# Two steps' attention scores in one block, and the attention values in a feed-forward PSUM bank

## The chip, the cores and the metric

The kernel runs on one core of a Trainium2 chip. The metric is device time in microseconds (us) for one execution, median of three runs. The core has five engines that work side by side, each through a queue of its own in program order: TensorE (PE, matrix products; its weight loads are listed as PEld), VectorE (DVE), ScalarE (ACT), GpSimd (POOL), and SyncE (SP), which here only issues DMAs. Products land in PSUM, which has eight banks of 512 fp32 columns by 128 partitions; ACT and DVE read them from there.

## What is computed

Top-k attention over 8 batches x 8 heads x 576 positions x 64 features, then a feed-forward block over the 4608 tokens. Everything is fp32 at the kernel's edge.

```python
scores = scale * np.matmul(q, k.transpose(0, 1, 3, 2))            # 576 x 576 for each batch and head
kth = np.partition(scores, -32, axis=-1)[..., -32:-31]            # the 32nd largest of each row
scores = np.where(scores >= kth, scores, -1e9)
scores = scores - scores.max(-1, keepdims=True)
attn = np.exp(scores); attn = attn / (attn.sum(-1, keepdims=True) + 1e-9)
x = (attn @ v).transpose(0, 2, 1, 3).reshape(4608, 512)
h = x @ w_in                                                      # 512 -> 2048
out = (h - np.tanh(h)) @ w_out                                    # 2048 -> 512
```

## The kernel before

**Steps.** Attention is cut into 144 steps. A step is one pair of heads by 128 query rows: the pair's two heads are `t` = 0 and 1. 576 is 4 x 128 + 64, so the last 64 query rows of two head pairs make a "rem" step of their own. Steps come in groups of two (`nq` = 2, two row blocks of one head pair) whose values are computed together; a unit of feed-forward work is 256 tokens (128 for a few), and is ready when the values of its four head pairs are there. One batch is 18 steps.

**The loop.** The order of all instructions is written out by the Python loop `for n in range(-4, NS + LAG)`; no scheduler moves them inside it. In turn n the loop issues work of several steps:

- `mask(n - 1)`: POOL makes the threshold (`tb`, L334), ACT a relu against it (L347), POOL a subtraction (L350) and a check (`bad`, L354).
- `search(n)`: DVE finds the 32nd largest score of each row. It folds the near half of the keys, read from PSUM (`ps`), with the far half, read from the SBUF copy (`sc`): L297 to L305; then rounds of MAX8 and MATCH_REPLACE8 (L309 to L319). Between the rounds lie the reciprocal of step n - 2 (`invert`, L389 on DVE), its scaling on ACT (`divide`, L396), and its 32x32 transposition on DVE (`turn_z`, L427).
- `spread_keys(n - 2)`: SP sends the transposed weights to DRAM and back into the layout that the value products want (`there`, then `et` or `spare`).
- `deal(0.4)`: a share of the waiting feed-forward work.
- `scores(n + 1)`: PE makes the scores of the next step (L267), ACT copies them to SBUF (L275).
- `expo(n - 1)`: ACT's exponentials with their sums (L370); POOL adds the epsilon (`rd`, L380).
- three times `deal(0.2)`, and the loads and transpositions of q and k and the loads of v that are due.

**Values.** `values(m)` runs five turns after its group's last step (`LAG`): ten pairs of products on PE (L492) into PSUM, and a copy by ACT into the unit's input `xT` (L512). From turn `NEAR` = 45 on it stands directly ahead of `scores`; before that, at the start of the turn.

**Feed-forward.** Work is dealt in items of equal PE time. `ffn_h` is one item of 8 products (16 records in the trace, since an fp32 product shows as two); two items fill a bank, and then ACT makes tanh (L555) and a copy (L556) from it, and POOL subtracts them (L557). `ffn_o` adds up one 128-token block of the output over 8 items in one bank; ACT copies it (L574) and SP stores it. `rate()` sets how many items a turn gets, from the turns at which units become ready.

**PSUM.** Eight banks: four for the scores of one step (`ps[P, 2, 2, 512]`: two heads by two halves of 288 keys), two in turn for `zt` (transpositions early on, and the values `av`), two in turn for the feed-forward (`h_ps`).

**Shapes of products.** Feed-forward products use all 128 rows and 128 columns of PE's array. Score products have 64 rows (the head's features), and two run side by side, one in each half of the rows; value products have 64 columns, and two run side by side in the halves of the columns. The trace names them 128\*128, 64\*128 and 128\*64 (64\*64 for the scores of rem steps).

Of the kernel before, what the change touches and what calls it, by code (L numbers as in the profile page):

```python
# [10 lines left out]
FP32 = mybir.dt.float32  # L11
# [10 lines left out]

NEAR = 45


# [26 lines left out]
def kernel(  # L52
# [49 lines left out]
    sc_ps = pool("sc_ps", 1, space=PS)  # L102
    zt_ps = pool("zt_ps", 2, space=PS)
    h_ps = pool("h_ps", 2, space=PS)

# [34 lines left out]
    def convert(piece, slot):  # L140


        j, i = piece // CD, piece % CD
        if j < WJ:
            src, dst = moe_w_in[i * P : (i + 1) * P, j * NW : (j + 1) * NW], w_in[j][:, i, :]
        else:
            r0 = ((j - WJ) * FJ + i) * P
            src, dst = moe_w_out[r0 : r0 + P, :], w_out[j - WJ][:, i, :]
        raw, shifted, _ = slot
        nc.sync.dma_start(flat(raw), src.bitcast(U32))  # L150
        nc.sync.dma_start(
            flat(shifted).bitcast(U8)[:, 0 : 8 * NW - 4], src.bitcast(U8)[:, 3 : 8 * NW - 1]
        )
# [7 lines left out]
        e = h_ps.tile([P, NW], FP32, tag="h", name="e")[:] if j < WJ else f[:]  # L161
# [12 lines left out]
        yield  # L174
# [56 lines left out]
    def turn_rows(name, b, hp):  # L231
# [7 lines left out]
        for c0, c1, w in ((0, J, P), (J, J + 1, R)):  # L239
            zt = zt_ps.tile([P, 512], FP32, tag="zt", name="zt")  # L240
            for c in range(c0, c1):
# [14 lines left out]
    rest = consts.tile([P, 2, S4 + Q], FP32, name="rest")  # L256

    def scores(n):
        g = steps[n]
        ps = sc_ps.tile([P, 2, 2, 512], FP32, tag="sc", name="scps")  # L260
        for s in range(2):
            ks = slice(s * S2, (s + 1) * S2)
            for i in range(2 if g.rem else 1):
                qs = slice(JP, S) if g.rem else slice(g.qt * P, (g.qt + 1) * P)
                rows = half(i) if g.rem else slice(0, P)
                for t in range(2):
                    nc.tensor.matmul(  # L267
                        ps[rows, t, s, 0:S2],
                        qT[g.b, g.hp + i][half(t), qs],
                        kT[g.b, g.hp + i][half(t), ks],  # L270
                        start=True,
                        stop=True,
                    )
        sc = scpool.tile([P, 2, 2, S2], FP32, tag="sc", name="sc")
        nc.scalar.copy(sc[:], ps[:, :, :, 0:S2])  # L275
        st[n] = dict(sc=sc, ps=ps)

    def search(n, exact, between):
# [5 lines left out]
        x = st[n]  # L284
        sc, ps = x["sc"], x.pop("ps")
        m = x["m"] = mpool.tile([P, 2, TOP], FP32, tag="m", name="m")
# [6 lines left out]
        else:  # L293
            top = x["top"] = tpool.tile([P, 2, S4 + Q], FP32, tag="top", name="top")
            near, far = ps[:, :, 0, 0:S2], sc[:, :, 1, :]
            a, b = half_max, ps[:, :, 0, S2 : S2 + S4]
            nc.vector.tensor_tensor(b, near[:, :, S4:], far[:, :, S4:], ALU.max)  # L297
# [151 lines left out]
    def turn_pe(n):  # L449
# [10 lines left out]
        for k0 in range(0, KC, J):  # L460
            kn = min(J, KC - k0)
            zt = zt_ps.tile([P, 512], FP32, tag="zt", name="zt")
            for k in range(kn):
# [13 lines left out]

    def values(n):


        g = steps[n]
        nq, u = g.nq, g.unit
        et = tiles(ets.pop(n), nq)
        w = nq * P
        av = zt_ps.tile([P, 2, N], FP32, tag="zt", name="av")
        for i in range(2 if g.rem else 1):
# [3 lines left out]
            for c in range(J + 1):  # L490
                for t in range(2):
# [5 lines left out]
                        stop=(c == J),  # L497
                    )
        if g.pe:
            rx = rxs.pop(n)  # L500
# [32 lines left out]
    def ffn_h(u, item):  # L533
# [3 lines left out]
        for f in range(item * per, (item + 1) * per):  # L537
            j, fo = f // FJ, (f % FJ) * P
            s = f * w % 512
            if s == 0:  # L540
                cur[u] = h_ps.tile([P, 512], FP32, tag="h", name="hps")
            for c in range(CD):
# [7 lines left out]
        if item % 2:  # L550
# [3 lines left out]
            g = u.g[-1][:, item % 4 // 2, :]  # L554
            nc.scalar.activation(th[:], cur[u][:], AF.Tanh)  # L555
            nc.scalar.copy(g, cur[u][:])  # L556
            nc.gpsimd.tensor_tensor(g, g, th[:], ALU.subtract)  # L557

    def ffn_o(u, i, part):
        if part == 0:  # L560
            cur[u] = h_ps.tile([P, DM], FP32, tag="h", name="ops")
        for f in range(2 * part, 2 * part + 2):
            o = f * u.n + i * P
            nc.tensor.matmul(  # L564
                cur[u][:],
                u.g[o // 1024][:, o % 1024 // 512, o % 512 : o % 512 + P],
# [6 lines left out]
        ot = thpool.tile([P, DM], FP32, tag="th", name="ot")  # L573
        nc.scalar.copy(ot[:], cur[u][:])  # L574
        for rows, dst in u.blocks[i]:
# [51 lines left out]
    def run(exact):  # L627
# [10 lines left out]
        for i, (b, hp) in enumerate(pairs):  # L638
            n = next(n for n, g in enumerate(steps) if (g.b, g.hp) == (b, hp))
            for x, name in enumerate("kq"):  # L640
                m = max(n - 5 + x, turned.get(name, -4))
                if b == 0 and not exact:
# [106 lines left out]

        for n in range(-4, NS + LAG):  # L750
            pe = here(-2) and steps[n - 2].pe
            def due():
                for m in (n - LAG, n - LAG + 1, n - LAG + 2):
                    if 0 <= m < NS and steps[m].last and steps[m].lag == n - m:
                        values(m)

            if n < NEAR:
                due()
            share, usable = rate(), converted[0]
# [15 lines left out]
            if n >= NEAR:  # L775
                due()
            if here(1):
                scores(n + 1)
            if pe:
# [20 lines left out]
    nc.vector.reduce_max(any_bad[:], bad[:].rearrange("p t n i -> p (t n i)"), axis=mybir.AxisListType.X)  # L800
    cnt = zt_ps.tile([P, 512], FP32, tag="zt", name="cnt")
    nc.tensor.matmul(cnt[0:1, 0:1], any_bad[:], ones[:], start=True, stop=True)
# [35 lines left out]
```

## Time and profile before

| | |
|---|---|
| median of 3 runs | 1512.03 us (1511.23 to 1512.41) |
| the profiled execution's own time | 1509.65 us |
| its span, first to last instruction | 1507.5 us |
| mean granted TensorE clock | 0.982 |
| busy, share of the span | PE 95%, DVE 86%, ACT 67%, POOL 58% |
| largest groups | `ffn_o` products 517.5 us, `ffn_h` products 466.7 us, score products 189.0 us, value products with 256 columns from `et` 62.3 us and from `spare` 54.5 us |
| ACT copy of a step's scores | 1114 ns, 144 times |

The median stands 2.4 us above the profiled execution's own time, and that stands 2.15 us above its span. "Busy" counts a matmul from its start to its modelled end, so that PE at 100% can still hold gaps between the starts of its products; those are read from the rows in order of time. A wait is idle time of an engine together with what released it.

### The profile page before, as it was taken

The page shows a single profiled execution, that of the slowest core. Times are in us where ns is not written, and L with a number is a line of the kernel's source. Part 1 is how long each engine was busy: PE and PEld are TensorE (multiplying, and loading weights), DVE is VectorE, ACT ScalarE, POOL GpSimd, SP SyncE. Part 2 cuts the span into 40 slices and gives each one's busy share as a digit, 9 for nine tenths or more (in the row PEclk, how much of TensorE's full clock was granted, in tenths as well). Part 3 has the DMA queues.
Part 4 walks back from the last instruction along what each step waited for, and adds up shares of the span by engine and source line. Part 5 has one row for each costly group of instructions (what it writes and reads, how often), then busy time and mean ns, then how long its engine had stood idle before and what let it go on. Part 6 is the DMA issues. An engine that isn't in the chain of part 4 may idle for free.

```text
span 1507.5 us, 25020 instructions
## 1 busy us (share of the span) xinstructions
PE 1426.5 (95%) x7332; PEld 908.2 (60%) x7332; DVE 1295.2 (86%) x4886; ACT 1004.9 (67%) x1813; POOL 879.1 (58%) x1370
## 2 busy tenths in 40 slices
PE   4667898999999999999999999999999999999998
PEld 2454656465666565656565665657575675656673
DVE  7999899999998999999989999899988989886100
ACT  4766777777776777777676676768676676766220
POOL 3777667566565575657565575747474664646120
PEclk9888999999999999999999999999999999999999
DMA  9954123657854685567655865466554766443400
GB/s 277 373 170 167 25 43 92 171 156 153 205 147 140 164 166 156 134 176 171 162 136 146 175 147 165 138 166 159 156 145 117 174 144 177 111 140 105 109 7 17
DMA packets 248563, 221.68 MB, mean 147 GB/s; under 512 B 190816, under 2 KB 197984, under 8 KB 241248
## 3 DMA queue, kind: packets, MB, share of 16 engines
q1 hardware_dynamic: 246640, 219.75, 56.0%
q8 instruction: 61, 1.00, 0.3%
q14 instruction: 86, 0.70, 0.2%
q10 hardware_dynamic: 1776, 0.22, 0.1%
HBM read 136.17 MB, written 83.76 MB: 146 GB/s over the span
## 4 chain that ended last, share of the span: by engine, by line
PE 74%; DVE 15%; ACT 4%; POOL 2%; DMA 2%; issue 1%; SPq 0%; ACTq 0%; DVEq 0%; POOLq 0%
PE ops L564 28%; PE hps L543 28%; PE av L492 9%; PE scps L267 8%; DVE m L316 3%; DVE top L309 2%; DVE rest L319 2%; DVE zx L427 2%; DVE ab L303 1%; DMA w_in<-in_k_dram 1%; DVE f L170 1%; PE zt L464 1%; DVE f L159 1%; DVE top L319 1%; DVE ab L298 1%
## 5 line engine op out<-in xcount | busy, mean ns | idle before, releaser
L564 PE MATMUL ops<-w_out,g 128*128 128x512 f32 x1152 | 517.5, 600 | 2.4 <-POOL bad L354 1.5
L543 PE MATMUL hps<-xT,w_in 128*128 128x256 f32 (+1 forms) x2176 | 466.7, 372 | 1.0 <-ACT g L556 0.9
L350 POOL TENSOR_TENSOR z<-sc,z 128x576 f32<-128x576 f32 x288 | 404.5, 1426 | 86.2 <-ACT z L347 86.2
L543 PEld LDWEIGHTS hps<-xT,w_in 128*128 128x128 f32 x2176 | 392.0, 192 | 75.8 <-issue 21.6
L564 PEld LDWEIGHTS ops<-w_out,g 128*128 128x128 f32 x1152 | 213.3, 191 | 262.3 <-issue 250.3
L347 ACT ACTIVATE z<-sc,tb 128x576 f32<-128x576 f32 x288 | 207.6, 769 | 141.9 <-POOL tb L334 141.2
L557 POOL TENSOR_TENSOR g<-g,th 128x512 f32<-128x512 f32 x144 | 183.6, 1277 | 145.7 <-ACT g L556 140.9
L396 ACT ACTIVATE z<-z,rd 128x576 f32<-128x576 f32 x252 | 180.7, 764 | 97.0 <-DVE rd L389 96.9
L370 ACT ACTIVATE z<-z,nb 128x576 f32<-128x576 f32 x288 | 221.6, 774 | 2.5 <-POOL z L350 2.4
L380 POOL TENSOR_SCALAR rd<-den 128x2 f32<-128x2 f32 x144 | 32.7, 227 | 312.9 <-ACT z L370 307.1
L267 PE MATMUL scps<-kT,qT 64*128 64x288 f32 (+1 forms) x1280 | 189.0, 447 | 18.4 <-DVE qT L237 8.2
L427 DVE STREAM_TRANSPOSE zx<-z 128x1152 f32<-128x1152 f32 x126 | 172.0, 1365 | 35.2 <-ACT z L396 34.6
L309 DVE MAX8 top<-ab 128x8 f32<-128x144 f32 x864 | 194.6, 295 | 0.0
L275 ACT COPY sc<-scps 128x1152 f32<-128x1152 f32 x144 | 160.4, 1114 | 41.8 <-PE scps L267 41.4
L316 DVE MAX8 m<-rest 128x8 f32<-128x168 f32 x576 | 161.6, 322 | 0.0
L267 PEld LDWEIGHTS scps<-kT,qT 64*128 64x128 f32 (+1 forms) x1280 | 102.4, 184 | 94.5 <-issue 19.9
L316 DVE MAX8 m<-top 128x8 f32<-128x144 f32 (+1 forms) x576 | 151.7, 305 | 0.0
L555 ACT ACTIVATE th<-hps 128x512 f32<-128x512 f32 x144 | 84.2, 585 | 64.5 <-PE hps L543 62.1
L303 DVE TENSOR_TENSOR ab<-scps,sc 128x576 f32<-128x576 f32 x144 | 107.6, 748 | 0.0
L297 DVE TENSOR_TENSOR scps<-scps,sc 128x288 f32<-128x288 f32 x144 | 64.6, 449 | 46.1 <-ACT sc L275 45.7
L354 POOL TENSOR_SCALAR bad<-top,tb 128x3 uint8<-128x3 f32 x288 | 95.0, 341 | 0.0
L492 PE MATMUL av<-et,vb 128*64 128x256 f32 (+1 forms) x640 | 76.8, 372 | 18.2 <-ACT et L467 18.2
(78 smaller groups left out, 1536.8 us busy)
## 6 DMA issues: line engine op xcount, KB each, us to landing
there<-zx SPq DMA_DIRECT2D x56, 1152.0 KB, 4.2
spare<-there SPq DMA_DIRECT2D x112, 288.0 KB, 4.7
et<-there SPq DMA_DIRECT2D x112, 288.0 KB, 5.2
kin<-in_k_dram SPq DMA_DIRECT2D x116, 72.0 KB, 2.9
vb<-in_v_dram SPq DMA_DIRECT2D x64, 128.0 KB, 5.9
out_dram<-ot SPq DMA_DIRECT2D x32, 256.0 KB, 3.3
qin<-in_q_dram SPq DMA_DIRECT2D x113, 72.0 KB, 3.7
there<-zx SPq DMA_DIRECT2D x14, 576.0 KB, 5.2
```

Of the source, the lines that this page charges most:

```text
L267: nc.tensor.matmul(ps[rows, t, s, 0:S2], qT[g.b, g.hp + i][half(t), qs], kT[g.b, g.hp + i][half(t), ks], start=True, stop=True,)
L309: nc.vector.max(top[:, t, o : o + 8], low[:, t, i, :])
L316: nc.vector.max(m[:, t, m8], seen[i][t])
L347: nc.scalar.activation(zv[:, t, :], scf[:, t, :], AF.Relu, bias=tb[:, t : t + 1], scale=-BIG)
L350: nc.gpsimd.tensor_tensor(zv[:, t, :], scf[:, t, :], zv[:, t, :], ALU.subtract)
L370: nc.scalar.activation(x["zv"][:, t, :], x["zv"][:, t, :], AF.Exp, bias=x["nb"][:, t : t + 1], scale=scale, accum_out=den[:, t : t + 1],)
L396: nc.scalar.activation(x, x, AF.Copy, scale=rds[n][:, g.i, t : t + 1])
L427: nc.vector.transpose(tiles(zx, g.nq)[:, :, :, g.i, :].rearrange("p c k j -> p k c j"), z[:].rearrange("p (k c j) -> p k c j", c=NG, j=G),)
L492: nc.tensor.matmul(av[half(t), 0, cols], vb[g.b, hp][:, t, c, :] if c < J else vr[g.b, hp][:, t, :], es[:, :, (J + 1) * t + c if c < J els ...
L543: nc.tensor.matmul(cur[u][:, s : s + w], w_in[j][:, c, fo : fo + P], u.xT[:, c, 0:w], start=(c == 0), stop=(c == CD - 1),)
L557: nc.gpsimd.tensor_tensor(g, g, th[:], ALU.subtract)
L564: nc.tensor.matmul(cur[u][:], u.g[o // 1024][:, o % 1024 // 512, o % 512 : o % 512 + P], w_out[f // FJ][:, f % FJ, :], start=(f == 0), sto ...
```

## The change

From turn 18 on (`PAIRS`), the scores of two steps are made in one go in every even turn, and none in the odd ones. The four score banks now hold, for each of the two steps and heads, keys 0 to 319 (`WIDE`); the remaining 256 keys of both steps go into the two `zt` banks. ACT's one copy of 1152 columns for a step becomes three, of 640, 256 and 256. DVE's scratch in the score banks moves to columns 320 to 463.

Since the `zt` banks are taken, the values are put into whichever of the two feed-forward banks is not in use, `hbs[last_hb[0] ^ 1]`. Values that would be due in an odd turn wait for the next even one, where a rem step's may join others in the same bank. From turn 45 on they stand directly ahead of the scores of two steps. `zt` and feed-forward banks are now four fixed tiles that `zt_bank()` and `h_bank()` hand out in turn. q and k are loaded and transposed one turn earlier.

```diff
-    zt_ps = pool("zt_ps", 2, space=PS)
-    h_ps = pool("h_ps", 2, space=PS)
+    zt_ps = pool("zt_ps", 1, space=PS)
+    h_ps = pool("h_ps", 1, space=PS)
+    zts = [zt_ps.tile([P, 512], FP32, name=f"zt{i}")[:] for i in range(2)]
+    hbs = [h_ps.tile([P, 512], FP32, name=f"hb{i}")[:] for i in range(2)]
+    last_zt, last_hb = [0], [0]
+    def zt_bank():
+        last_zt[0] ^= 1
+        return zts[last_zt[0]]
+    def h_bank():
+        last_hb[0] ^= 1
+        return hbs[last_hb[0]]
...
+    def scores_of_two(n):
+        ps = sc_ps.tile([P, 2, 2, 512], FP32, tag="sc", name="scps")
+        ends = [x.rearrange("p (i k) -> p i k", i=2)[:, :, 0 : S - WIDE] for x in zts]
+        for i in range(2):
+            products(steps[n + i], lambda rows, t: ps[rows, i, t, 0:WIDE], slice(0, WIDE))
+            products(steps[n + i], lambda rows, t: ends[t][rows, i, :], slice(WIDE, S))
+        for i in range(2):
+            sc = scpool.tile([P, 2, 2, S2], FP32, tag="sc", name="sc")
+            scf = sc[:].rearrange("p t s k -> p t (s k)")
+            nc.scalar.copy(scf[:, :, 0:WIDE], ps[:, i, :, 0:WIDE])
+            for t in range(2):
+                nc.scalar.copy(scf[:, t, WIDE:S], ends[t][:, i])
+            st[n + i] = dict(sc=sc, near=ps[:, i])
...
-            near, far = ps[:, :, 0, 0:S2], sc[:, :, 1, :]
-            a, b = half_max, ps[:, :, 0, S2 : S2 + S4]
+            near, far = ps[:, :, 0:S2], sc[:, :, 1, :]
+            a, b = half_max, ps[:, :, WIDE : WIDE + S4]
...
-    def values(n):
+    def values(*ns):
+        if steps[ns[0]].pe:
+            bank = zt_bank().rearrange("p (a n) -> p a n", a=2)
+            weigh(ns[0], bank)
+            put_values(ns[0], bank)
+            return
+        bank = hbs[last_hb[0] ^ 1].rearrange("p (a n) -> p a n", a=2)
+        for x, n in enumerate(ns):
+            weigh(n, bank[:, x:])
+        for x, n in enumerate(ns):
+            put_values(n, bank[:, x:])
...
-                m = max(n - 5 + x, turned.get(name, -4))
+                m = max(n - 6 + x, turned.get(name, -4))
...
-                    at(n - 3 + x, turn)
-                    turned[name] = n - 3 + x
+                    at(n - 4 + x, turn)
+                    turned[name] = n - 4 + x
...
+        due = {}
         for m, g in enumerate(steps):
             if g.last:
-                begun.setdefault(g.unit, m + g.lag)
+                x = m + g.lag
+                if not g.pe:
+                    x += max(x - PAIRS, 0) % 2
+                    due.setdefault(x, []).append(m)
+                begun.setdefault(g.unit, x)
                 if m in done:
-                    ready[g.unit] = m + g.lag + g.pe
+                    ready[g.unit] = x + g.pe
...
-            if here(1):
-                scores(n + 1)
+            if here(1) and n + 1 not in st:
+                if n >= PAIRS and here(2):
+                    scores_of_two(n + 1)
+                else:
+                    scores(n + 1)
```

The values that PE transposes early on (`pe` steps of the first batch) keep to the `zt` banks. The product that counts rows for a repeat (`cnt`, L802 before), which the compiled program had behind all feed-forward products, now stands behind the values of turn 144.

More of the change, by code (lines that the diff above doesn't have):

```diff
@@ L23 @@
 NEAR = 45
+PAIRS = 18
+WIDE = 320
 class Step:
@@ L159, in convert @@
         nc.vector.tensor_scalar(fu, hi, 20, 0x7FF, ALU.logical_shift_right, ALU.bitwise_and)
-        e = h_ps.tile([P, NW], FP32, tag="h", name="e")[:] if j < WJ else f[:]
+        e = h_bank() if j < WJ else f[:]
         nc.scalar.activation(e.bitcast(I32), fu, AF.Relu, bias=e896[:], scale=2.0**23)
@@ L239, in turn_rows @@
         for c0, c1, w in ((0, J, P), (J, J + 1, R)):
-            zt = zt_ps.tile([P, 512], FP32, tag="zt", name="zt")
+            zt = zt_bank()
             for c in range(c0, c1):
@@ L256, with products @@
     rest = consts.tile([P, 2, S4 + Q], FP32, name="rest")
+    def products(g, out, ks):
+        for i in range(2 if g.rem else 1):
+            qs = slice(JP, S) if g.rem else slice(g.qt * P, (g.qt + 1) * P)
+            rows = half(i) if g.rem else slice(0, P)
+            for t in range(2):
+                nc.tensor.matmul(
+                    out(rows, t),
+                    qT[g.b, g.hp + i][half(t), qs],
+                    kT[g.b, g.hp + i][half(t), ks],
+                    start=True,
+                    stop=True,
+                )
     def scores(n):
-        g = steps[n]
         ps = sc_ps.tile([P, 2, 2, 512], FP32, tag="sc", name="scps")
@@ L262, in scores @@
             ks = slice(s * S2, (s + 1) * S2)
[L263 to L273, printed above, removed]
+            products(steps[n], lambda rows, t: ps[rows, t, s, 0:S2], ks)
         sc = scpool.tile([P, 2, 2, S2], FP32, tag="sc", name="sc")
         nc.scalar.copy(sc[:], ps[:, :, :, 0:S2])
-        st[n] = dict(sc=sc, ps=ps)
+        st[n] = dict(sc=sc, near=ps[:, :, 0, :])
+    def scores_of_two(n):
[8 more added lines that the diff above has]
+            nc.scalar.copy(scf[:, :, 0:WIDE], ps[:, i, :, 0:WIDE])
+            for t in range(2):
+                nc.scalar.copy(scf[:, t, WIDE:S], ends[t][:, i])
+            st[n + i] = dict(sc=sc, near=ps[:, i])
     def search(n, exact, between):
         x = st[n]
-        sc, ps = x["sc"], x.pop("ps")
+        sc, ps = x["sc"], x.pop("near")
         m = x["m"] = mpool.tile([P, 2, TOP], FP32, tag="m", name="m")
@@ L461, in turn_pe @@
             kn = min(J, KC - k0)
-            zt = zt_ps.tile([P, 512], FP32, tag="zt", name="zt")
+            zt = zt_bank()
             for k in range(kn):
@@ L476, in in_order, with weigh @@
         return x.rearrange("p (a i j) -> p i a j", a=NG, i=nq)
-    def values(n):
+    def values(*ns):
[9 more added lines that the diff above has]
+            put_values(n, bank[:, x:])
+    def weigh(n, av):
         g = steps[n]
-        nq, u = g.nq, g.unit
+        nq = g.nq
         et = tiles(ets.pop(n), nq)
         w = nq * P
-        av = zt_ps.tile([P, 2, N], FP32, tag="zt", name="av")
         for i in range(2 if g.rem else 1):
@@ L498, in values, with put_values @@
                     )
+    def put_values(n, av):
+        g = steps[n]
+        nq, u = g.nq, g.unit
+        w = nq * P
         if g.pe:
@@ L540, in ffn_h @@
             if s == 0:
-                cur[u] = h_ps.tile([P, 512], FP32, tag="h", name="hps")
+                cur[u] = h_bank()
             for c in range(CD):
@@ L554, in ffn_h @@
             g = u.g[-1][:, item % 4 // 2, :]
-            nc.scalar.activation(th[:], cur[u][:], AF.Tanh)
-            nc.scalar.copy(g, cur[u][:])
+            nc.scalar.activation(th[:], cur[u], AF.Tanh)
+            nc.scalar.copy(g, cur[u])
             nc.gpsimd.tensor_tensor(g, g, th[:], ALU.subtract)
@@ L560, in ffn_o @@
         if part == 0:
-            cur[u] = h_ps.tile([P, DM], FP32, tag="h", name="ops")
+            cur[u] = h_bank()
         for f in range(2 * part, 2 * part + 2):
@@ L564, in ffn_o @@
             nc.tensor.matmul(
-                cur[u][:],
+                cur[u],
                 u.g[o // 1024][:, o % 1024 // 512, o % 512 : o % 512 + P],
@@ L573, in ffn_o @@
         ot = thpool.tile([P, DM], FP32, tag="th", name="ot")
-        nc.scalar.copy(ot[:], cur[u][:])
+        nc.scalar.copy(ot[:], cur[u])
         for rows, dst in u.blocks[i]:
@@ L748, in deal, with of_step @@
             credit = min(credit, 1.0)
-        for n in range(-4, NS + LAG):
+        def of_step(n):
+            if n in due:
+                values(*due[n])
+        for n in range(-4, NS + LAG + 1):
             pe = here(-2) and steps[n - 2].pe
[L752 to L755, printed above, removed]
             if n < NEAR:
-                due()
+                of_step(n)
             share, usable = rate(), converted[0]
@@ L775, in run @@
             if n >= NEAR:
-                due()
-            if here(1):
-                scores(n + 1)
+                of_step(n)
+            if here(1) and n + 1 not in st:
[3 more added lines that the diff above has]
+                    scores(n + 1)
             if pe:
@@ L800 @@
     nc.vector.reduce_max(any_bad[:], bad[:].rearrange("p t n i -> p (t n i)"), axis=mybir.AxisListType.X)
-    cnt = zt_ps.tile([P, 512], FP32, tag="zt", name="cnt")
+    cnt = zt_bank()
     nc.tensor.matmul(cnt[0:1, 0:1], any_bad[:], ones[:], start=True, stop=True)
```

## The prediction

> **What bounds the kernel now.** I read the head of the page and the shares of its chain first. (Columns: engine, busy us, share of the span, instructions; then the chain.)
>
> ```profile
> PE 1426.5 (95%) x7332; PEld 908.2 (60%) x7332; DVE 1295.2 (86%) x4886; ACT 1004.9 (67%) x1813; POOL 879.1 (58%) x1370
> PE 74%; DVE 15%; ACT 4%; POOL 2%; DMA 2%; issue 1%; SPq 0%; ACTq 0%; DVEq 0%; POOLq 0%
> ```
>
> PE carries the end, DVE the second share. Which of them, and where, is read from busy time by stretch: I cut the steady part at DVE's L297 into stretches of 9 and 18 steps. (Start:end, length, then busy us of PE, PEld, DVE, ACT, POOL, granted clock, DMA share, GB/s.)
>
> ```profile
> 290.00:368.00 78.00, 74.61 (x390) 45.72 (x389) 77.66 (x302) 58.46 (x106) 50.40 (x83) 1.00 0.65 163
> 948.00:1120.00 172.00, 172.00 (x861) 111.05 (x860) 158.98 (x604) 122.77 (x221) 104.51 (x164) 1.00 0.61 155
> ```
>
> In the first stretch (steps 27 to 35) DVE has no idle time: 78/9 = 8.67 us is its floor for a step, and PE has 3.4 us to spare. In the second (steps 99 to 116) a step takes 172/18 = 9.56 us, PE is never idle, and DVE has 13 us to spare. So a PE saving is worth nothing before about step 36, and from about step 45 (448 us) on it is worth its full size, as long as a step stays above 8.67 us.
>
> Next I read PE in order of time, for what a block of another shape costs it. (Start us, us, engine, line, names, records; first line from the chain.)
>
> ```profile
> 1472.95 27.48 PE ops L564 x64
> 711.17 7.13 PE L564 MATMUL ops<-w_out,g 128*128 128x512 f32 x16
> 718.24 1.24 PE L267 MATMUL scps<-kT,qT 64*128 64x288 f32 x8
> 719.41 1.12 PE L564 MATMUL ops<-w_out,g 128*128 128x512 f32 x2
> 942.62 1.95 PE L492 MATMUL av<-et,vb 128*64 128x256 f32 x16
> 944.93 1.24 PE L267 MATMUL scps<-kT,qT 64*128 64x288 f32 x8
> ```
>
> A 512-column record takes 27.48/64 = 0.429 us in a steady run. Start to start, the 16 from 711.17 should take 6.87 and take 7.07; the scores, four side-by-side pairs of 288 columns, should take 4 x 0.429 x 288/512 = 0.97 and take 719.41 - 718.24 = 1.17. So a block of scores loses 0.20 at each side, 0.40 in all. Values ahead of scores: ten pairs of 256 columns are 2.15, and 942.62 to 944.93 is 2.31. One change of shape between neighbours is about 0.2 us, a little less on entry into values.
>
> **Part 1, fewer changes of shape.** In the compiled order of PE's main part there are 400 such changes before and 282 after: 144 blocks of scores become 82, and 84 of values become 77. 118 x 0.2 = 23.6, less 1 for the cheaper entries: 23 us of PE time. The products' columns stay (320 + 256 = 576), and so do those products. Thirteen of the removed blocks (5 us) lie in turns 18 to 44, where DVE has no room; I count 2 of those 5. **-20 us.** A change between 64\*128 and 64\*64 inside a block (14 new ones) is taken at the same 0.2; with nothing for them it is -23.
>
> **Part 2, values in the idle feed-forward bank.** Before, values had two banks of their own, and PE never waited for them. Now PE's first value product waits until ACT has emptied the bank that the feed-forward left last; behind it on PE stand the scores of two steps and all feed-forward work, and DVE waits for the scores. How late ACT is there, the trace shows at the values of 963.21:
>
> ```profile
> 959.31 0.59 ACT L556 COPY g<-hps 128x512 f32<-128x512 f32 x1
> 959.99 1.27 POOL L557 TENSOR_TENSOR g<-g,th 128x512 f32<-128x512 f32 x1 [0.72 <-ACT g L556]
> 961.25 0.58 POOL L334 TENSOR_SCALAR tb<-m 128x1 f32<-128x1 f32 x2
> 961.58 1.44 ACT L347 ACTIVATE z<-sc,tb 128x576 f32<-128x576 f32 x2 [1.68 <-POOL tb L334]
> 962.93 1.43 ACT L396 ACTIVATE z<-z,rd 128x576 f32<-128x576 f32 x2
> 963.21 1.95 PE L492 MATMUL av<-spare,vb 128*64 128x256 f32 x16
> 964.26 0.57 ACT L555 ACTIVATE th<-hps 128x512 f32<-128x512 f32 x1
> 964.74 0.56 ACT L556 COPY g<-hps 128x512 f32<-128x512 f32 x1
> ```
>
> Read it downwards as one chain: ACT empties one bank (to 959.90), POOL subtracts, and only then makes the thresholds of the next step; ACT does L347 and L396 of that step, and only then empties the next bank, to 965.30. PE had ended that bank 1.66 us (half a bank, 8 records of 256 columns) before the values began at 963.21. In the changed kernel those values would stand still for 2.09 us.
>
> From 448 us on the trace has ten values that begin half a bank after an `ffn_h` bank ended. Values' start against the end of that bank's L556, they would have waited 2.43, 2.04, 2.65, 2.77, 2.09, 2.09, 2.93 and 1.41 us, and twice nothing: mean 1.84. In the changed order, from turn 46 to 142, 14 of 49 blocks of values have just this place: 14 x 1.84 = **+26 us**. Bounds: 0 if ACT is always ahead, 14 x 2.93 = 41 if never. Five more come half a bank after an `ffn_o` bank, which has one copy instead of two (one such place waits 0.87 us, another is free): **+2**. Where the values begin a whole bank later (3.4 us) or more, every place from 448 us on has the bank free for 1.6 us or longer: nothing. After those, the next feed-forward product goes into the values' bank, and needs L512 (0.37 us); the scores of two steps, 2.1 us on PE, cover it, else it is about 0.5 each.
>
> [...] If every one of the 49 blocks had to wait out an emptying (1.05 us by the last two rows above), that would be +51 in place of +28; the rows say that most places are free.
>
> **Part 3, no scores in odd turns.** The 1.6 us block that stood between feed-forward banks is gone there, so the bank after next is wanted 3.44 us (16 records) after the one in it ended. The trace's `ffn_h` banks are empty 1.1 to 4.9 us after their last product (one of 6.8 apart), and between 448 and 1120 us 17 of 71 take over 3.44. Some 18 odd turns carry a full run of `ffn_h`. A quarter of them by about 0.7 is 3; all 18 by the longest excess of 1.5 would be 27, none 0. **+3.**
>
> **Part 4, ACT.** A copy of 1152 columns takes 1.11; of 256, 0.37 (L512); 640 columns, between the 512-column copy's 0.57 and that by their slope, 0.68. Three copies are 1.42: +0.3 a step, 38 us of ACT in all, hidden by ACT's 28% of idle time, and at full price +38 if ACT were the bound. The second step's copies stand ahead of `expo`, so L370, `rd`, `tb`, L396 and DVE's L427 move by 1.4 in every other step. POOL's `rd` usually has room before DVE's reciprocal, but the stretch to 448 us has no room on DVE: 13 pairs by 0 to 0.9. **+2** (0 to 12).
>
> **No cost:** loads and turns of q and k a turn earlier (the same 8 DMAs per head pair, past `there`/`et` on SP); `et`'s writes may wait on SP for values that are a turn later, but they are needed three turns on, and PE's L492 waits only 1.1 us for DMA in the whole run (else up to 5.2, the landing time of `et`, per group); DVE's arithmetic, the same columns; fixed tiles, which issue nothing; `cnt`, whose input was ready at 1395.8, before the values of 1397.7 that it now follows.
>
> **Sum:** -20 + 26 + 2 + 3 + 2 = +13 on the execution's own 1509.65, 1522.7; the median stood 2.4 above that, so **1525**.
>
> **Rivals.**
> - *ACT is ahead in even turns* (faster). An odd turn has no score copy and no wait of ACT for PE's scores, so its banks empty 1.1 us earlier and the chain of part 2 may have run off when the values come. It decides at one number: an `ffn_h` bank empty within 1.7 us of its last product. For: in two of the ten places it was. Against: POOL's subtraction holds up the thresholds however early ACT was. Then only part 1 is left with the small terms: -20, 1492.
> - *ACT's chain becomes the bound of `ffn_h` stretches* (slower still). After a wait the chain runs in series: values, scores, ACT's copies, L370, emptying, L557, `tb`, L347, L396, emptying. Part 2 at 2.9 and part 3 at 0.7 in all 18: -20 + 41 + 2 + 13 + 6 = +42, at most 1554; half way, 1540. For: ACT and POOL wait for one another longest in the table of waits (L380 behind L370, 307 us). Against: PE never waited for this chain before.
> - *Gains and waits cancel*: waits of 1.2 instead of 1.84 (17 us), and no more: about 1512.
>
> **Chances.** Forecast (waits of 1.5 to 2.5 us at those places) 0.45, the slower rival 0.22, faster 0.25, cancel 0.08. The likeliest case alone spans 1515 to 1533. The range leaves out some 0.1 at each side: 1496, which takes in the faster case with some of its waits, to 1543. A run of this kernel can't tell less than about 0.2%, 3 us, from no change. Faster 0.25, same 0.08, slower 0.67.
>
> **What would show it.** Right: PE's L267 blocks near 82, with 0.2 lost at each side; PE idle ahead of L535 (the values), released by ACT's L605, about 2 us in some 14 places, all in `ffn_h` runs; PE busy below 100% in stretches that had it. Wrong: no idle time there (faster rival), or DVE waiting in odd turns ahead of L459, or as PE's releaser after step 45.

## The result, and the profile after

The changed kernel takes 1594.19 us (median of 4 runs, 1593.33 to 1596.94) against 1512.22 (1511.23 to 1512.73) on the same chip: a ratio of 1.055 with an interval of 1.053 to 1.056, or 82 us slower. The profiled execution has a span of 1595.1 us, 87.6 above that of before. The prediction had the sign, but 1525 us and a range that ended at 1543.

Line numbers from here on are those of the changed kernel: L535 are the value products, L277 the scores, L592 `ffn_h`, L613 `ffn_o`, L604 and L605 ACT's tanh and copy that empty an `ffn_h` bank, L606 POOL's subtraction, L366 `tb`, L379 the relu, L428 the scaling (`divide`), L561 the copy into `xT`. An `ffn_h` item of a unit of 256 tokens is 4 products, 8 records, so that two items fill a bank in 16 records or 3.44 us, as the prediction has it; the 8 products named at the start hold for units of 128 tokens.

The head of the page, as before (engine, busy us, share, records):

```profile
PE 1434.9 (90%) x7332; PEld 930.5 (58%) x7332; DVE 1295.0 (81%) x4886; ACT 1022.1 (64%) x2061; POOL 878.7 (55%) x1370
```

PE has the same 7332 records; its 8.4 us more are records that run slower, and in the other 79 us it is simply idle. ACT's 17 us more are the three copies in place of one. The same two groups of steps as in the prediction, 27 to 35 and 99 to 116, by busy time (start:end, length, busy us of PE, PEld, DVE, ACT, POOL, granted clock, DMA share, GB/s):

```profile
301.00:386.00 85.00, 73.61 (x376) 46.33 (x376) 79.36 (x302) 60.58 (x126) 49.80 (x80) 0.94 0.64 158
1009.00:1186.00 177.00, 168.19 (x847) 110.42 (x846) 157.64 (x602) 123.18 (x254) 104.52 (x164) 0.99 0.61 149
```

Steps 27 to 35 take 9.4 us each instead of 8.7, and DVE, which had no idle time there, now has 5.6 us. Steps 99 to 116 take 9.83 instead of 9.56 us, and PE, which was never idle, now is for 9 us. The table of waits names the releaser (engine, tile and line waiting, what ended the wait, us in total, times, longest us):

```profile
DVE scps L329 <- ACT sc L305: 117.8, 43, 6.9
PE hb L535 <- ACT g L605: 46.7, 18, 4.4
PE hb L535 <- ACT ot L623: 12.2, 5, 2.9
PE hb L592 <- ACT g L605: 11.7, 10, 1.6
PE hb L592 <- ACT xT L561: 7.0, 7, 2.4
```

The four rows of PE are new but for one wait of 0.9 us: values wait for ACT to empty a feed-forward bank (59 us, 23 times), and feed-forward products wait for a bank (19 us). DVE's wait for a score copy was this before:

```profile
DVE scps L297 <- ACT sc L275: 45.7, 45, 3.7
```

It is the same lateness passed on: in e5 below, with the same copies but without the shared bank, it is 36.8 us. One place where values wait, in order of time (start us, us, engine, line, records, and in brackets the idle time before and what ended it):

```profile
636.46 0.58 ACT L604 ACTIVATE th<-hb 128x512 f32<-128x512 f32 x1
636.94 0.57 ACT L605 COPY g<-hb 128x512 f32<-128x512 f32 x1
637.59 1.28 POOL L606 TENSOR_TENSOR g<-g,th 128x512 f32<-128x512 f32 x1 [0.72 <-ACT g L605]
638.86 0.58 POOL L366 TENSOR_SCALAR tb<-m 128x1 f32<-128x1 f32 x2
639.20 1.44 ACT L379 ACTIVATE z<-sc,tb 128x576 f32<-128x576 f32 x2 [1.69 <-POOL tb L366]
641.56 1.44 ACT L428 ACTIVATE z<-z,rd 128x576 f32<-128x576 f32 x2 [0.92 <-DVE rd L421]
642.90 0.58 ACT L604 ACTIVATE th<-hb 128x512 f32<-128x512 f32 x1
643.38 0.57 ACT L605 COPY g<-hb 128x512 f32<-128x512 f32 x1
644.01 3.25 PE L535 MATMUL hb<-et,vb 128*64 128x256 f32 x16 [3.36 <-ACT g L605]
648.14 0.37 ACT L561 COPY xT<-hb 128x256 f32<-128x256 f32 x1 [4.19 <-PE hb L535]
```

This is the chain that the prediction read in the trace of before: emptying, POOL's subtraction, `tb`, L379, L428, next emptying. ACT itself stands idle twice in it (1.69 and 0.92 us), because L379 and L428, which stand ahead of the next emptying in its queue, wait for POOL and DVE. What had not been in the trace of before is that PE stands at the end of it, for 3.36 us. And the 16 records of values then take 3.25 us instead of 1.95. The granted clock (the first number after the five engines) shows why:

```profile
640.00:643.00 3.00, 0.64 (x3) 0.21 (x2) 3.00 (x20) 2.08 (x4) 2.94 (x3) 1.00 0.26 75
643.00:646.00 3.00, 1.99 (x12) 1.30 (x14) 2.35 (x7) 0.95 (x2) 1.72 (x3) 0.75 0.97 224
646.00:649.00 3.00, 3.00 (x18) 1.56 (x17) 0.00 (x0) 0.37 (x1) 0.00 (x0) 0.68 1.04 221
649.00:652.00 3.00, 3.00 (x21) 2.29 (x18) 0.30 (x1) 2.17 (x6) 0.00 (x0) 1.00 0.51 126
```

After the idle stretch the clock falls to half for 3.4 us, from 644.48 to 647.89. Scores are hit in the same way. The first row is a half of a step's scores after values that did not wait, the second, at a granted clock of 0.50 from 746.88 on, after values that had waited 2.65 us at 745.64:

```profile
704.01 0.81 PE L277 MATMUL scps<-kT,qT 64*128 64x320 f32 x4
...
746.97 1.44 PE L277 MATMUL scps<-kT,qT 64*128 64x320 f32 x4
```

**Where the 88 us are.** I took PE's products in order of time and, for each, the time from its start to the next start, less its columns at 0.429 us per 512. Excesses over 0.5 us are counted as waits, smaller ones as pace and changes of shape. How records that run side by side are paired moves up to 4 us between the first two rows; it hardly touches the waits.

| | steps 18 to 44 | from step 45 | sum |
|---|---|---|---|
| changes of shape, and what small excesses are left | -5.8 | -16.9 | -22.7 |
| pace of value and score products | +6.9 | +12.8 | +19.7 |
| waits ahead of values (7 and 16 places, none before) | +19.4 | +43.2 | +62.6 |
| waits ahead of `ffn_h` that follows values or scores | +4.8 | +7.9 | +12.7 |
| waits between two `ffn_h` banks | +1.1 | +11.2 | +12.3 |
| other waits | -0.7 | +1.4 | +0.7 |

With 3.4 us ahead of step 18 this is 88.7; the spans differ by 87.6, the rest being at the ends. The granted clock is at half for 58.0 us between steps 18 and 143, against 3.4 before; that is where the second row comes from.

**Which values wait.** From step 45 on there are 52 blocks of values. 15 begin one feed-forward item (1.72 us, half an `ffn_h` bank) after an `ffn_h` bank ended: 13 of them wait, 35.7 us in all. 5 begin one item after an `ffn_o` bank: 3 wait, 7.5 us. The other 32 begin a whole `ffn_h` bank or more after it, and none waits. Before step 45, five of the seven that wait begin two items (3.44 us, a whole `ffn_h` bank) later.

### The profile page after: what moved, and what is told of

Its sections match the earlier page's. It is cut to its first block, busy times and chain, and to the rows that moved or that the text cites. A ratio compares the mean times of both kernels' runs of the same rounds, so it can differ in the third digit from the quotient of the medians.

```text
span 1595.1 us, 25183 instructions
## 1 busy us (share of the span) xinstructions
PE 1434.9 (90%) x7332; PEld 930.5 (58%) x7332; DVE 1295.0 (81%) x4886; ACT 1022.1 (64%) x2061; POOL 878.7 (55%) x1370
## 5 line engine op out<-in xcount | busy, mean ns | idle before, releaser
L613 PE MATMUL hb<-w_out,g 128*128 128x512 f32 x1152 | 509.9, 597 | 3.9 <-ACT g L605 2.7
L592 PE MATMUL hb<-xT,w_in 128*128 128x256 f32 (+1 forms) x2176 | 463.0, 372 | 18.8 <-ACT g L605 9.3
L592 PEld LDWEIGHTS hb<-xT,w_in 128*128 128x128 f32 x2176 | 396.3, 194 | 86.6 <-ACT g L605 13.1
L613 PEld LDWEIGHTS hb<-w_out,g 128*128 128x128 f32 x1152 | 216.0, 191 | 264.7 <-issue 248.2
L379 ACT ACTIVATE z<-sc,tb 128x576 f32<-128x576 f32 x288 | 207.6, 769 | 141.4 <-POOL tb L366 129.6
L606 POOL TENSOR_TENSOR g<-g,th 128x512 f32<-128x512 f32 x144 | 183.1, 1274 | 134.5 <-ACT g L605 129.7
L428 ACT ACTIVATE z<-z,rd 128x576 f32<-128x576 f32 x252 | 180.9, 765 | 108.5 <-DVE rd L421 108.5
L412 POOL TENSOR_SCALAR rd<-den 128x2 f32<-128x2 f32 x144 | 32.7, 227 | 393.8 <-ACT z L402 390.7
L459 DVE STREAM_TRANSPOSE zx<-z 128x1152 f32<-128x1152 f32 x126 | 172.0, 1365 | 29.0 <-ACT z L428 28.9
L277 PE MATMUL scps<-kT,qT 64*128 64x320 f32 (+3 forms) x728 | 135.9, 502 | 13.6 <-DVE qT L251 8.0
L535 PE MATMUL hb<-spare,vb 128*64 128x256 f32 (+1 forms) x896 | 82.9, 333 | 46.8 <-ACT g L605 37.4
L305 ACT COPY sc<-scps 128x640 f32<-128x640 f32 x124 | 87.9, 709 | 47.5 <-PE scps L277 46.5
L604 ACT ACTIVATE th<-hb 128x512 f32<-128x512 f32 x144 | 84.8, 589 | 49.4 <-PE hb L592 46.9
L535 PEld LDWEIGHTS hb<-spare,vb 128*64 128x64 f32 x896 | 49.7, 146 | 83.7 <-ACT g L605 44.4
```

What stands on the lines that cost most here:

```text
L277: nc.tensor.matmul(out(rows, t), qT[g.b, g.hp + i][half(t), qs], kT[g.b, g.hp + i][half(t), ks], start=True, stop=True,)
L379: nc.scalar.activation(zv[:, t, :], scf[:, t, :], AF.Relu, bias=tb[:, t : t + 1], scale=-BIG)
L428: nc.scalar.activation(x, x, AF.Copy, scale=rds[n][:, g.i, t : t + 1])
L459: nc.vector.transpose(tiles(zx, g.nq)[:, :, :, g.i, :].rearrange("p c k j -> p k c j"), z[:].rearrange("p (k c j) -> p k c j", c=NG, j=G),)
L535: nc.tensor.matmul(av[half(t), 0, cols], vb[g.b, hp][:, t, c, :] if c < J else vr[g.b, hp][:, t, :], es[:, :, (J + 1) * t + c if c < J els ...
L592: nc.tensor.matmul(cur[u][:, s : s + w], w_in[j][:, c, fo : fo + P], u.xT[:, c, 0:w], start=(c == 0), stop=(c == CD - 1),)
```

## The experiments

Times are medians; "before" is the kernel before on the same chip (1510.42 to 1512.06 by group of runs). Theories: **W**, PE waits for the feed-forward bank, and runs at half pace after it; **P**, the scores of two steps cost by themselves; **D**, the rest of the change (fixed tiles, loads and values a turn earlier or later); **C**, ACT's chain in series is what PE waits for, wherever the values stand; **B**, the wait is the length of one emptying; **K**, half pace follows from standing still.

### Parts alone

**e1: the change without both of its main parts.**

```diff
-        bank = hbs[last_hb[0] ^ 1].rearrange("p (a n) -> p a n", a=2)
+        bank = zt_bank().rearrange("p (a n) -> p a n", a=2)
...
-                if n >= PAIRS and here(2):
-                    scores_of_two(n + 1)
-                else:
-                    scores(n + 1)
+                scores(n + 1)
```

> Scores step by step again and values in the zt banks again; left of the change: values held to even turns, q and k a turn earlier, fixed tiles, cnt's place. Theory W (PE waits ahead of the values for ACT to empty a feed-forward bank, 61 us in 24 places after 211 us in the changed kernel's trace, and runs the values at half pace after it, 22 us): nothing of it is left, 1512 us, at most 6 more. Rival P (the pairs of steps cost it, by ACT's three copies and by scores that come late to DVE): also 1512. Rival D (it is the later values and earlier turns that put DVE, ACT and SP out of step): 1530 or more.

Measured: 1517.57, ratio 1.0042 (1.0025 to 1.0059). The rest of the change costs 5.5 us, as more waiting of scores for the score banks between steps 18 and 45 (17.1 us of such waits against 9.0). D is small.

**e2: values in the feed-forward bank, scores one step at a time.** Only the second half of e1's diff.

> Scores step by step, values in the idle feed-forward bank in even turns. Theory W: the waits ahead of the values and the half pace are all here, and nothing is saved on changes of shape: 1512 + 60 to 83, so 1570 to 1600. Rival P: the cost belongs to the pairs, at most 1530. Rival D: as e1, 1530 or more in both.

Measured: 1565.53, ratio 1.0354 (1.0336 to 1.0372). 48 us more than e1, by the bank alone. This is a few us below the range that W named, and far above P's. Waits ahead of values are 10.2 us before step 45 and 32.7 after it, in 22 places. With the scores of two steps, in the changed kernel, they are 19.4 and 43.2 in 23 places: the two parts together cost more than each by itself.

**e7: the kernel before with three copies on ACT instead of one.**

```diff
-        nc.scalar.copy(sc[:], ps[:, :, :, 0:S2])
+        nc.scalar.copy(sc[:, :, 0, :], ps[:, :, 0, 0:S2])
+        for t in range(2):
+            nc.scalar.copy(sc[:, t, 1, :], ps[:, t, 1, 0:S2])
```

> The kernel before, with ACT's one copy of a step's 1152 score columns cut into three of 576, 288 and 288; nothing else. It prices the copies of part 4 alone. If ACT's time is covered there, as the prediction has it: 1512 to 1516. If ACT is close to a bound (theory P): its added 0.3 us a step shows in part or in full, 1520 to 1555.

Measured: 1511.54 against 1510.42, ratio 1.0010 (1.0001 to 1.0020), which is 1.5 us (0.2 to 3.0). ACT's added time is covered.

**e4 and e5: scores of two steps, but values in their own banks.** In odd turns those two banks are free. e4 changes the bank and the parity alone:

```diff
-        bank = hbs[last_hb[0] ^ 1].rearrange("p (a n) -> p a n", a=2)
+        bank = zt_bank().rearrange("p (a n) -> p a n", a=2)
...
-                    x += max(x - PAIRS, 0) % 2
+                    x += max(x - PAIRS + 1, 0) % 2
```

> Scores of two steps in even turns, values in odd turns and in the zt banks, which are free by then. Theory W: no wait for a feed-forward bank; the values now stand alone, so of the 23 us that fewer changes of shape save some 49 x 0.2 = 10 are given back: 1512 - 13 = 1499, 1495 to 1510. Rival P: the pairs cost what they cost, 1540 or more. Rival D: 1530 or more.

Measured: 1894.55, ratio 1.254. The values are a turn later than e4's buffers allow: they stand behind `spread_keys`, which by then has put the next group's weights into the same `et`. So e4 multiplies with the later group's weights, and PE waits for DMAs that were only just issued (331 us in 21 places). It says nothing on the two theories; e5 mends it by issuing the products at the start of the turn, with ACT's copy at its old place.

> The changed kernel, with the scores of two steps as there, but the values made in odd turns, at the turn's start, in the two banks that held the last 256 keys of the scores (free by then); no value product shares a bank with the feed-forward. If waiting for a feed-forward bank is what costs (theory W): the waits ahead of values go, about 61 us of them in the changed kernel, and the saving of shapes stays, less some 10 us for values that now stand alone between feed-forward products: 1500 to 1512. If the scores of two steps cost by themselves (theory P: three copies on ACT, scores that come late for one step and early for the other): 1530 or more, with DVE waiting for ACT's copies.

Measured: 1522.38, ratio 1.0088 (1.0069 to 1.0106), 12 us above the kernel before on its chip where the changed kernel was 82 above, with no wait of values for a feed-forward bank. W holds for 70 of the 82 us. The 12 us that are left put it 10 above the range that W named; P's 1530 was not reached, and DVE waits less for ACT's copies than before. What grew is PE's wait for DVE to release the score banks, 6.7 us in 6 places before:

```profile
DVE scps L329 <- ACT sc L305: 36.8, 31, 3.3
PE scps L277 <- DVE top L337: 22.2, 11, 4.7
```

The bank costs 48 us beside scores of one step (e2 against e1) and 70 beside scores of two: some 20 us belong to neither part alone.

### Which bank, which moment

**e3 and e8: values begun only at the end of a whole bank.** e3 is the changed kernel, e8 has the scores of e2:

```diff
         def of_step(n):
+            nonlocal credit
             if n in due:
+                while work and age[0] < 2 and work[0][0] <= usable:
+                    work.pop(0)[2]()
+                    credit -= 1
                 values(*due[n])
```

(`age` counts the feed-forward items since the bank in use was handed out.)

> The changed kernel, but values are begun only when two or more feed-forward items lie between them and the idle bank's last product (one more item is dealt first where it was one). Theory W: the half-bank places and their half pace go, most of 83 us; left are waits of the next feed-forward bank (H to H 12 us, scores to H 7 us) against 20 saved: 1512 to 1540. Rival P or D: 1570 or more, since pairs and lateness are all there.

> The scores of one step at a time as before, the values in the idle feed-forward bank in even turns, but begun only when at least two feed-forward items (a whole bank) have been issued into the bank in use. If half a bank is the only place that waits, as the prediction has it (theory W): no waits ahead of values, 1520 to 1530. If an emptying is often more than a bank late (theory C): 1545 to 1570, the waits still there ahead of the values or moved to the next feed-forward bank.

Measured: e3 1570.46, ratio 1.0385 (1.0366 to 1.0404); e8 1551.03, ratio 1.0271 (1.0253 to 1.0290). Both miss W's figure, and e8 lies in C's range. (e3's 1570 is also the least that P or D named; e1, e5 and e7 speak against those.) Half a bank is not the only place that can wait. In e3 the rows that had been 46.7, 11.7 and 12.2 are these:

```profile
PE hb L538 <- ACT g L609: 21.6, 16, 2.7
PE hb L595 <- ACT g L609: 16.1, 11, 1.7
PE hb L538 <- ACT ot L628: 9.9, 5, 2.9
```

(Some lines were added ahead, so L538, L609, L595 and L628 are L535, L605, L592 and L623.) Values that begin a whole bank later wait less, 35.0 us against 62.6 by the count of the table above, but still in 21 places, and the feed-forward waits more. At those places ACT is more than a bank behind, which is C.

**e6 and e10: ACT empties first.** In even turns the first 0.4 of the feed-forward work, with its emptying, is issued ahead of `mask(n - 1)`; e6 from turn 18, e10 from 46 on top of e9 (below).

```diff
+            early = n >= PAIRS and n % 2 == 0 and not pe
+            if early:
+                deal(0.4)
             if here(-1):
                 mask(n - 1, exact)
...
-            deal(0.0 if pe else 0.4)
+            deal(0.0 if pe or early else 0.4)
```

> The changed kernel, but in even turns from 18 on the first 0.4 of the turn's feed-forward work, with ACT's emptying of its banks, is issued ahead of mask(n - 1), so that ACT empties a bank before the relu that needs POOL's threshold, and before divide. If ACT is late for the values because these stand ahead of the emptying in its queue (theory C, the chain), the waits ahead of the values fall from 61 us to 30 or less and the time to 1560 or below. If the waits are only the length of an emptying behind a full bank (theory B), they stay within 10 us of 61 and the time within 1585 to 1600, or above, since mask is later for DVE.

> The kernel that begins at turn 46, with the first 0.4 of the even turns' feed-forward work issued ahead of mask(n - 1), as in e6 but only from 46 on. In e6 the stretch from step 45 to the end took 1082 us, against 1124 in the changed kernel and 1059 in the kernel before, with no wait ahead of values left. If the chain of ACT and POOL ahead of the emptying (theory C) is what PE waits for, this gives 1525 to 1545. If e6 gained there only because it had fallen behind earlier, 1560 or more.

Measured: e6 1568.29, ratio 1.0390 (1.0371 to 1.0408); e10 1533.12, ratio 1.0151 (1.0132 to 1.0170), within its range. In e6 the waits ahead of values fall to 22.4 us, as C has it, but the time misses C's 1560, because steps 18 to 44 became worse (271 us against 257 in the changed kernel and 237 before); from step 45 on there is no wait ahead of values left in it. The rows of e6:

```profile
PE hb L535 <- ACT g L605: 15.0, 5, 5.2
DVE zx L459 <- ACT z L428: 91.1, 54, 7.8
```

The first row was 46.7; the second, 28.9 in the changed kernel, is the price: the relu and the scaling now stand behind the emptying, and DVE waits for them. In e10 the waits ahead of values after step 45 are 1.4 us instead of e9's 24.9, but those ahead of `ffn_h` and between its banks grow from 15.5 to 33.8. The row of the values in e9, then in e10:

```profile
PE hb L538 <- ACT g L608: 14.4, 7, 3.0
```

```profile
PE hb L538 <- ACT g L608: 0.4, 1, 0.4
```

So it is the work ahead of the emptying in ACT's queue that PE waits for. The chain can be cut at one link, and then holds at another.

**e9: the change from turn 46 only** (`PAIRS = 46`, values in their own banks before it).

> The changed kernel with PAIRS = 46: scores of two steps, and values in the feed-forward bank, only from turn 46 on; the turns before it as in the kernel before. The changed kernel loses about 20 us between steps 18 and 45, where the prediction counted 2. If that loss is lasting, this one is at 1568 to 1580. If it only moves the work (feed-forward that is not done there would be done in DVE's idle time later), it stays at 1588 or above.

Measured: 1546.66, ratio 1.0245 (1.0226 to 1.0263), below both figures expected, and 35.5 us above the kernel before on its chip. So the turns 18 to 45 cost some 46 us of the 82, though they themselves are only 20 us longer: in e9 the waits ahead of values after step 45 are 24.9 us in 11 places, against 43.2 in 16. The kinds of place do not explain it: values that begin one item after the idle bank ended are 18 in e9 and 20 in the changed kernel. More of these wait there, and longer; why a late start does this stays open.

**e12: PE kept busy ahead of the values.** Two products into a free bank, which nothing reads, ahead of each block of values from turn 46:

```diff
+                if n > NEAR and n in due:
+                    fill = zt_bank()
+                    for c in range(2):
+                        nc.tensor.matmul(
+                            fill[:, 0:512], w_in[0][:, c, 0:P], w_out[0][:, c, :],
+                            start=(c == 0), stop=(c == 1),
+                        )
                 of_step(n)
```

> The changed kernel, with two products of 128x128 by 512 columns (4 records, 1.72 us) that nothing reads ahead of every block of values from turn 46 on, so that PE stands still less long before them. 49 x 1.72 = 84 us more work on PE, of which about 28 should lie in the waits that were there. If the half pace of value products comes from PE standing still (theory K), the loss of pace in blocks of values and scores falls back to that of the kernel before (some 10 us less) and the time is 1634 to 1646. If it comes from the bank that they share with the feed-forward, the loss of pace stays and the time is 1647 to 1658.

Measured: 1631.76, ratio 1.0808. There were 52 such places, 208 records or 89 us of added work, for 38 us more time, 2 us below the range that K named. A place of e12 (L832 are the added products):

```profile
664.76 1.88 PE L832 MATMUL zt<-w_out,w_in 128*128 128x512 f32 x4
667.38 1.95 PE L535 MATMUL hb<-spare,vb 128*64 128x256 f32 x16 [0.73 <-ACT g L605]
```

In the changed kernel the values of this place, at 668.02, waited 2.44 us and took 3.38; here the wait is shortened to 0.73 us, and the values keep their 1.95. From step 45 on the waits ahead of values fall from 43.2 to 14.1 us, the loss of pace in value products from 9.5 us above the kernel before to less than 1, and the time at half clock from 34.1 to 3.4 us, though the values use the same bank. K holds: here the half pace came from standing still.

### What the saved shapes are worth

**e11: e5 from turn 46** (`PAIRS = 46` in e5).

> Scores of two steps and values in their own two banks in odd turns, as in e5, but from turn 46 on. e5 lost 9.6 us on the kernel before between steps 18 and 45 and gained 3 from there to step 126. If these add, 1506 to 1514: the change of shape that is saved is worth about 9 us without the shared bank, and is mostly given back as PE's waits for the score banks. If the scores of two steps cost as much from 46 on, 1518 to 1525.

Measured: 1513.01, ratio 1.0019 (1.0008 to 1.0030), inside the first range. From step 45 on, the changes of shape and other small excesses are some 5 us less than before, and the waits 13.8 us against 4.7. The first is less of a saving than in the changed kernel, since values that stand alone have a change on each side; the second are scores that wait for DVE to release the score banks, 12.4 us in 6 places against 0.9.

**e13 and e14: e11 with 0.2 and 0.4 of a turn's feed-forward ahead of the scores.**

```diff
             deal(0.0 if pe else 0.4)
+            later = 0.0 if pe or n < PAIRS or n % 2 else 0.2
+            deal(later)
...
-            deal(0.8 if pe else 0.2)
+            deal(0.8 if pe else 0.2 - min(later, 0.2))
...
-            deal(0.0 if pe else 0.2)
+            deal(0.0 if pe else 0.2 - max(later - 0.2, 0.0))
```

> e11 (scores of two steps, values in their own banks in odd turns, from turn 46), with 0.2 of a turn's feed-forward work moved ahead of the scores in even turns. In e11 the changes of shape cost some 10 us less than before from step 45 on, but PE waits 11 us more for DVE to release the score banks, because the scores come earlier in its order. If that is where the saving went, the waits shrink to 5 us or less and the time falls to 1500 to 1508, below the kernel before. If the scores then come too late for DVE, its wait for ACT's copies (31.5 us in e11) grows by 10 or more and the time is 1511 or above.

> As e13, with 0.4 of the turn's feed-forward work moved ahead of the scores. PE's waits for the score banks should be gone altogether; the scores are 1.8 us later than in e13, so that DVE's wait for ACT's copies grows. Where PE has the bound (from step 45 on, some 0.5 to 0.9 us of DVE's room per step), half of the delay is covered: 1500 to 1512; if DVE's lateness is passed on to the values and the feed-forward, 1515 or above.

Measured: e13 1513.53, ratio 1.0019 (1.0010 to 1.0028); e14 1544.41, ratio 1.0218 (1.0204 to 1.0232). Both miss the gain that was hoped for and take the worse of the two ways named ahead, with DVE waiting longer for the scores. In e13 the waits for the score banks halve (6.8 us), values wait 4.6 instead of 0.8, and the time stays. DVE's wait for the score copy in e13 and in e14, against 31.5 in e11:

```profile
DVE scps L329 <- ACT sc L305: 50.8, 31, 3.7
```

```profile
DVE scps L329 <- ACT sc L305: 92.0, 37, 5.2
```

In e14 the values wait in turn (29.8 us in 14 places), nearly all of it for ACT's copies of the scores out of the two banks that they share here:

```profile
PE zt L539 <- ACT sc L307: 27.5, 18, 3.5
```

It is the changed kernel's wait once more, with scores in the place of the feed-forward. Of the three places in a turn that were tried for the scores of two steps, the first (e11) is too early for the banks, the last (e14) too late for DVE, and the one between (e13) gains nothing. No version tried beats the kernel before.

## Why the prediction was wrong

**The sign was right, and so was the kind of wait.** PE's L277 blocks, the idle time ahead of L535 and its releaser L605 are as foretold; that all of it lies in `ffn_h` runs and after step 45 is not. The forecast's sum was +13, the measured one +82 (88 between the two profiles). Of the 75 us between +13 and 88, the steps below account for nearly all: pace after waits 19.7, places before step 45 19.4, the size of the waits from there on 15, the next feed-forward product 12.7, and part 3 with 9.

**Part 1 was right**: -20 against -22.7, to the 4 us named above. It took 5 us for steps 18 to 44 and discounted them to 2; 5.8 is measured. Three rows of the changed kernel show one joined block:

```profile
704.01 0.81 PE L277 MATMUL scps<-kT,qT 64*128 64x320 f32 x4
...
705.60 0.63 PE L277 MATMUL zt<-kT,qT 64*128 64x256 f32 x4
706.16 10.57 PE L613 MATMUL hb<-w_out,g 128*128 128x512 f32 x24
```

706.16 - 704.01 = 2.15 for both steps, whose columns are 1.94: one loss of 0.2 where two blocks had two.

**Part 2 is the step that failed**, four times over.
- *Places before step 45 were counted at nothing*, since DVE had no room there while PE had some to spare. DVE's floor covers more work on PE, but not a wait that DVE itself stands behind: values, then scores, then ACT's copies, then DVE. Measured: 19.4 us of waits in 7 places, steps 18 to 44 longer by 20 us, and by e9 some 46 in all.
- *The size of a wait, 1.84 us at 14 places and +2 for five `ffn_o` places*: the places were counted nearly right (they are 15 and 5), but from step 45 on they wait 35.7 and 7.5 us, 43.2 against 28, or 2.4 us for each of the 15. "Nothing" for values a whole bank later held there, at 32 blocks; it did not hold before step 45, nor in e3 and e8, where it is made the rule. The lags were taken from a trace in which PE never waited; that ACT's grow once each wait delays the scores and copies behind it fits the numbers, but was not shown apart. In e9, where the change begins at turn 46, the sum of 24.9 us is near the 28 by luck: 15.5 us at 13 `ffn_h` places, 1.2 each, and 9.4 at four `ffn_o` places.
- *"The scores of two steps cover" the next feed-forward product in the values' bank*: 12.7 us measured. L561 stands behind other work in the same queue as the other emptyings.
- *A wait was priced at its length.* Of the pace of products after it nothing was said: 19.7 us, in 58.0 us at half clock.

**Part 3** was +3 against 12.3. The bounds given, 0 to 27, held it; the quarter of the turns that I took was too few, as the banks are emptied later than in the trace of before.

**Part 4** was right: +2, and e7 has 1.5 for the copies alone. What was put at *no cost* was not quite free: e1 has 5.5 us for the later values, the earlier loads and the fixed tiles together.

**The rivals.** The slower one, ACT's chain in series, had the mechanism: it is the chain of the rows at 636.46, and e3, e6, e8 and e10 bear it out. Its price of +42 left out the steps before 45 and the pace. The argument against it, that PE never waited for this chain before, was no argument: before, PE had no place in the chain. The +51 that I weighed against part 2's +28 has every one of 49 blocks wait out an emptying of 1.05 us. That it is nearer than my 28 to the 62.6 of all places, and to the +48 of e2 against e1, is luck: 23 blocks wait, 2.7 us each.

## What to carry to other kernels

Before two kinds of work share a bank, follow the queue of the engine that empties it: whatever stands ahead of the emptying there, with what that waits for, becomes part of the wait (after step 45 the waits ahead of values were 24.9 us in e9, and 1.4 in e10, which empties first). A lag read from a trace in which nobody waits for it holds for that order of work alone: read as 1.84 us a place, it was 2.4 in the changed kernel and 1.2 in e9. Price a stall of the matrix engine with the slow products that follow it (19.7 us here), and do not count a stretch as covered because another engine is at its floor, if that engine is at the end of the chain that is delayed (19.4 us of waits in steps 18 to 44, counted at nothing).

## What the runs showed of the hardware

Many waits of PE in mid-kernel were followed by a granted clock of a half. I took the waits ahead of value products after step 18 in six runs (the changed kernel, e2, e3, e8, e9, e12), and looked for a microsecond with a granted clock under 0.6 in the 7 us that followed: none of 42 waits of 0.5 to 1.5 us had one, 2 of 27 of 1.5 to 2.3, and 30 of 40 above 2.3.

Where a wait lay decided too. In the traces of these six runs and of the kernel before, the granted clock was whole or half, and it changed only at points that lay a whole multiple of 3.413 us apart. I cut the six runs at these points, from step 18 to step 143, and took PE's idle time by the modelled ends of its records. Of 2035 windows at whole clock in which PE was idle for less than 1.6 us, none was followed by a window at half clock; of 25 with 1.6 to 2.0 us, 5 were; of 40 with 2.0 us or more, all 40. Of the wait of 2.65 us ahead of 745.64, 2.17 us lay in one window (PE's busy time is the second number after the stretch, its clock the first after the five engines):

```profile
743.47:746.88 3.41, 1.24 (x40) 1.24 (x40) 3.41 (x14) 2.12 (x4) 3.41 (x5) 1.00 0.02 3
746.88:750.29 3.41, 3.41 (x20) 2.39 (x17) 0.77 (x2) 0.33 (x2) 0.18 (x1) 0.50 0.74 291
750.29:753.71 3.42, 3.42 (x20) 2.75 (x17) 1.43 (x3) 3.34 (x9) 0.00 (x0) 1.00 0.14 59
```

The wait of 2.71 us ahead of 587.64 was split between two, and the clock stayed whole:

```profile
583.04:586.45 3.41, 1.89 (x9) 1.33 (x7) 3.41 (x20) 2.70 (x4) 3.00 (x6) 1.00 0.55 145
586.45:589.86 3.41, 2.22 (x20) 1.35 (x20) 3.20 (x9) 1.14 (x3) 2.63 (x4) 1.00 0.72 141
589.86:593.28 3.42, 3.42 (x24) 2.53 (x23) 0.00 (x0) 1.88 (x5) 0.00 (x0) 1.00 0.42 69
```
